# Opening of a fused attention and mixer kernel: smaller weight loads, more dummy products, one score moved

## The chip, the cores and the metric

The kernel runs on one core of a Trainium2 chip. The metric is the device time of one execution in microseconds (us), as the median of several runs. About 0.2% is the smallest difference that a measurement of this kernel tells from none.

## The reference

For each of 8 batches, attention over 12 heads with 448 tokens and 64 numbers a head, with a sigmoid in place of the softmax, and behind it a mixer block with two small networks, one over tokens and one over channels:

```python
scores = scale * np.matmul(q, k.transpose(0, 1, 3, 2)) - np.log(S)
attn = 1.0 / (1.0 + np.exp(-scores))
x = np.matmul(attn, v)                      # (8, 12, 448, 64), then (8, 448, 768)
h = np.maximum(x.transpose(0, 2, 1) @ w_tok1, 0.0) @ w_tok2
u = x + h.transpose(0, 2, 1)
h2 = np.maximum(u @ w_ch1, 0.0) @ w_ch2
return u + h2
```

`w_tok1` is 448 x 256, `w_ch1` 768 x 1536 and `w_ch2` 1536 x 768. Inputs and output are float32; the products are done in float16.

## The kernel before

The order of all work is written out by hand: the kernel's code lists the instructions, and each engine takes its own in that order. Semaphores for the data dependences are set by the framework.

The work goes in 24 cycles, three units (of four heads) for each of the 8 batches. A cycle computes seven scores with `qk(b, u, j)`: four products of 64 x 64 weights on TensorE into one of two score buffers in PSUM, then one sigmoid on ScalarE (L194) into `att`. Beside the scores of one unit stand the value products of the unit before (`av`), its transposition (`xtrans`, `xtrans_dma`), the token network (`tok1`, `ytrans`) and the channel network of the batch before (`ch1`, `ch2` and, from the third batch on, forms with fewer products).

The opening, about the first 64 us, differs from the steady part. Its pieces, in order:

- **Start.** `keep_warm(16)` gives TensorE 16 dummy products of 256 columns (the tile `heat`) while the first unit of `q` arrives. VectorE and ScalarE cast that unit (L1041, L1042). TensorE transposes `q` and the first two blocks of `k` (`tp_q`, `tp_k`), three more dummies follow, and the first scores start. Further `keep_warm` calls stand between the scores of cycle 0.
- **Cycles 0 to 2** (first batch) take their order from the list `between`. Behind them comes a stretch of single lines (L1102 to L1123) with cycle 3 (second batch, unit 0) and the first three blocks of `ch1`, the first product with `w_ch1`, held in `c1`. Of the six row blocks of `c1`, `ch1(0, cb, 0, 4)` uses blocks 0, 3, 1 and 4; blocks 2 and 5 follow in the loop at L1121.
- **Cycles 4 and 5** (second batch, units 1 and 2; the loop at L1146) hold the rest of `ch1` for the first batch. In each, `ch1_pair` does two blocks at once in 64-row steps: `turn0` has six steps of four products, `turn1` six more with the two PSUM banks swapped. Before the change the order is score 1, all of `turn0`, score 2, value products, score 3, value products, score 4, four steps of `turn1`, score 5, two steps, score 6. Cycle 5 ends with the first products that use `c2`, the other channel weight (L584). The transposed `q` and `k` of the third batch's units 1 and 2 are made in cycle 5 by VectorE copies (L129) and transposing DMAs on SP's queue (L142).

All loads of inputs and weights are issued by GpSimd (POOL), which casts them to float16 on the way, in one list (L945 to L1002). `load(b, t, src, u0, u1)` issues two transfers, one for each half of the partitions. The list goes: first batch; the token weights `w1` (two transfers, and one for its last 64 rows in partitions 0 to 63) and `w2s`; second batch's units with `load_c1(0)` (columns 0 to 767 of `c1`) and `load_c1(1)` among them; third batch's unit 0; `load_c2(0)`; third batch's units 1 and 2; `load_c2(1)`; third batch's first `v`. Partitions 64 to 127 of `w1`'s fourth block are set to zero first (L951) and loaded at L1189, in cycle 4. Later loads stand behind a small copy on POOL (`gate`, L1199, L1127, L1342), which waits for a transposing DMA or an output.

`turn_over(ps)` is a VectorE copy of one column from a PSUM bank; products into that bank that stand behind it in the order wait for it. It is used in the steady part, where a score stands within such steps.

Of the kernel before, what the change touches and what calls it, by code (L numbers as in the profile page):

```python
# [21 lines left out]
NJ = 7  # L22
NP = 64
NU = 3
# [6 lines left out]
def kernel(  # L31
# [11 lines left out]
    nc = tc.nc  # L43
# [5 lines left out]
    NDB = D // 128  # L49
    NCB = CC // 128  # L50
    N_CYCLES = NU * B
    N_FIRST = 4
# [13 lines left out]
    w1 = pc.tile([128, 4, TT], FP16, name="w1")  # L66
    w2 = pc.tile([128, 2, NJ, NP], FP16, name="w2")
    c1 = pc.tile([128, NDB, CC], FP16, name="c1")
# [12 lines left out]
    def xu(b):  # L81
        return xus[b % 2] if b else xu_0
# [5 lines left out]
    def bank(shape, dtype, name):  # L88

        if opening_banks:  # L90
            n = opening_banks.pop(0)
        else:
            n = at_bank[0]
            at_bank[0] = (n + 1) % 4
        return pp.tile(shape, dtype, tag=f"m{n}", bufs=1, name=name)
# [17 lines left out]
    def load(b, t, src, u0, u1):  # L113

        for g in range(2):
            dst = raw_tile(b, t)[64 * g : 64 * g + 64, u0:u1, :, :, :]
            heads = src[b, 6 * g + 2 * u0 : 6 * g + 2 * u1]
            nc.gpsimd.dma_start(
                out=dst.rearrange("p u hi j e -> p (u hi) (j e)"),
                in_=heads.rearrange("h (p j) e -> p h (j e)", j=NJ),  # L120
            )
# [60 lines left out]
    def qk(b, u, j):  # L182
        att[b, u, j] = pa.tile([128, 2, S], FP16, tag="att", bufs=10, name=f"att_{b}_{u}_{j}")
        ps = pp.tile([128, 2, 512], FP32, tag="qk", bufs=2, name=f"qk_{b}_{u}_{j}")
        for g in range(2):
            for hi in range(2):
                nc.tensor.matmul(  # L187
                    out=ps[64 * g : 64 * g + 64, hi, 0:S],
                    lhsT=tr[b, "k"][64 * hi : 64 * hi + 64, u, j, 64 * g : 64 * g + 64],
                    rhs=tr[b, "q"][64 * hi : 64 * hi + 64, u, :, 64 * g : 64 * g + 64],  # L190
                    start=True,
                    stop=True,
                )
        nc.scalar.activation(  # L194
            out=att[b, u, j][:, :, :],
            in_=ps[:, :, 0:S],
            func=SIGMOID,
            bias=bias_t[:, :],
            scale=att_scale,
        )  # L200
# [7 lines left out]
    def av(b, u, j0=0, j1=NJ, banks=None):  # L208
        if j0 == 0:
            xa[b, u] = banks or [  # L210
                bank([128, 512], FP32, f"xa_{b}_{u}_{g}")
                for g in range(2)
            ]
        ps = xa[b, u]
        for j in range(j0, j1):
            for g in range(2):
                for hi in range(2):
                    nc.tensor.matmul(  # L218
                        out=ps[g][64 * hi : 64 * hi + 64, 0:S],
                        lhsT=raw[b, "v"][64 * g : 64 * g + 64, u, hi, j, :],  # L220
                        rhs=att[b, u, j][64 * g : 64 * g + 64, hi, :],
                        start=(j == 0),
                        stop=(j == NJ - 1),
                    )
        if j1 == NJ:
            for g in range(2):
                nc.vector.tensor_copy(  # L227
                    out=xu(b)[:, u, g, 0:S], in_=ps[g][:, 0:S]
                )
            if NU * b + u >= N_CYCLES - 2:  # L230
                nc.vector.memset(xu(b)[:, u, :, S:512], 0.0)
            elif NU * b + u >= N_FIRST:
                nc.vector.tensor_copy(
                    out=xu(b)[:, u, :, S:512], in_=xu(b)[:, u, :, S - 64 : S]
                )
# [157 lines left out]
                    skip_group_check=loose,  # L393
                )

    def ch1_pair(b, cb):

        ps = [bank([128, 512], FP32, f"c1_{b}_{cb + p}") for p in range(2)]

        def step(turn, n):  # L400
            quads(
                ps,
                S,
                turn,
                lambda p, part, m: c1[
                    part, BY_UNIT[n], 128 * (cb + p) + m : 128 * (cb + p) + m + 64
                ],
                lambda p, part: ut(b, BY_UNIT[n])[part, 0:S],
                n == 0,
                n == NDB - 1,  # L410
            )

        def end():
            for p in range(2):
                ch1_out(b, cb + p, ps[p])

        turns = [[lambda t=t, n=n: step(t, n) for n in range(NDB)] for t in range(2)]
        return turns[0], turns[1], end
# [207 lines left out]
    turn_bank = {}  # L626
# [223 lines left out]
    def turn_over(ps):  # L850

        nc.vector.tensor_copy(out=turned[:, :], in_=ps[:, 0:1])
# [75 lines left out]
    for g, queue in enumerate((nc.scalar, nc.sync)):  # L928
        queue.dma_start(
            out=first_q[64 * g : 64 * g + 64].rearrange("p hi j e -> p hi (j e)"),  # L930
            in_=q[0, 6 * g : 6 * g + 2].rearrange("h (p j) e -> p h (j e)", j=NJ),
# [16 lines left out]
    nc.vector.memset(bias_t[:, :], att_bias)  # L948
    for b in range(2):
        nc.vector.memset(xu(b)[:, :, :, S:512], 0.0)  # L950
    nc.vector.memset(w1[64:128, 3, :], 0.0)  # L951
    load_first_k(2, NJ)
    load(0, "q", q, 1, 2)
    load(0, "k", k, 1, 2)
# [3 lines left out]
    tok_rows = moe_w_tok1.rearrange("(p j) t -> j p t", j=NJ)  # L958
    for par in range(2):
        part = slice(64 * par, 64 * par + 64)  # L960
        nc.gpsimd.dma_start(
            out=w1[part, 0:3, :],
            in_=tok_rows[0:6].rearrange("(t par) p c -> par p t c", par=2)[par],
        )
    nc.gpsimd.dma_start(out=w1[0:64, 3, :], in_=tok_rows[NJ - 1])
    load(0, "v", v, 1, 2)
    nc.gpsimd.dma_start(
        out=w2s[:, :, :], in_=moe_w_tok2.rearrange("(tc t) s -> t tc s", tc=2)
# [2 lines left out]
    load(1, "q", q, 0, 1)  # L971
    load(1, "k", k, 0, 1)

    def load_c1(half):
        cols = slice(CC // 2 * half, CC // 2 * half + CC // 2)
        nc.gpsimd.dma_start(
            out=c1[:, :, cols],
            in_=moe_w_ch1.rearrange("(db d) c -> d db c", db=NDB)[:, :, cols],
        )

    def load_c2(half):
        cols = slice(DH * half, DH * half + DH)
        nc.gpsimd.dma_start(
            out=c2[:, :, cols],
            in_=moe_w_ch2.rearrange("(cb c) d -> c cb d", cb=NCB)[:, :, cols],
        )

    load(1, "q", q, 1, 2)
    load(1, "k", k, 1, 2)
    load_c1(0)  # L990
    load(1, "v", v, 0, 1)
    load(1, "q", q, 2, NU)
    load(1, "k", k, 2, NU)
# [1 line left out]
    load(1, "v", v, 1, NU)  # L995
    load(2, "q", q, 0, 1)
    load(2, "k", k, 0, 1)
    load_c2(0)
    load(2, "k", k, 1, NU)
    load(2, "q", q, 1, NU)  # L1000
    load_c2(1)
    load(2, "v", v, 0, 1)  # L1002

# [22 lines left out]
    def keep_warm(n):  # L1026
        for _ in range(n):
            nc.tensor.matmul(
                out=heat[0][:, 0:256],
                lhsT=warm[:, 0:128],  # L1030
                rhs=warm[:, :],
                start=True,
                stop=True,
            )
# [1 line left out]

    nc.scalar.activation(out=gate[:, 0:1], in_=bias_t[:, :], func=SIGMOID)
    heat[0] = bank([128, 512], FP32, "heat")
    keep_warm(16)

    nc.vector.tensor_copy(out=raw_tile(0, "q")[:, 0, :, 0:4, :], in_=first_q[:, :, 0:4, :])  # L1041
    nc.scalar.activation(  # L1042
        out=raw_tile(0, "q")[:, 0, :, 4:NJ, :], in_=first_q[:, :, 4:NJ, :], func=COPYF
# [102 lines left out]
    for c, cb in ((N_FIRST, 3), (N_FIRST + 1, 8)):  # L1146
        b, u = divmod(c, NU)
        before = divmod(c - 1, NU)
        ahead = divmod(c + 1, NU)
        copies = []  # L1150

        def whole(cb):
            for d in range(0, NDB, 3):
                ch1(0, cb, d, d + 3)
                if copies:
                    copies.pop(0)()

        turn0, turn1, end = ch1_pair(0, cb)
        if c > N_FIRST:
            qk(b, u, 0)  # L1160
        qk(b, u, 1)
        for f in turn0:
            f()
        qk(b, u, 2)
        av(*before, 0, 4)
        qk(b, u, 3)
        av(*before, 4, NJ)
        if c - 1 in ON_DMA:
            xtrans_dma(*before)
        qk(b, u, 4)  # L1170
        for f in turn1[:4]:
            f()
        qk(b, u, 5)
        for f in turn1[4:]:
            f()
        end()
        qk(b, u, 6)
        if u == 2:
            copies = by_unit(2, 1)
        whole(cb + 2)  # L1180
        if c - 1 not in ON_DMA:
            xtrans(*before)
        for t in ("k", "q"):
            pe_transpose(ahead[0], t, ahead[1])
        whole(cb + 3)
        if c == N_FIRST:
            tok1(*before)
            whole(cb + 4)
            nc.gpsimd.dma_start(out=w1[64:128, 3, :], in_=tok_rows[NJ - 1])  # L1189
            ytrans(*before)  # L1190
        else:
            for w, f in pieces_ch2(0, by_half[:2]):
                f()
                if copies:
                    copies.pop(0)()
            while copies:
                copies.pop(0)()

            nc.gpsimd.tensor_copy(out=gate[:, :], in_=tr[2, "q"][:, 1, NJ - 1, 126:128])  # L1199
            load(2, "v", v, 1, NU)  # L1200
            gated_loads(b)
# [19 lines left out]
    for c in range(2 * NU, ONE_RUN):  # L1221
        b, u = divmod(c, NU)
# [170 lines left out]
    for c in range(ONE_RUN, N_CYCLES):  # L1393
        b, u = divmod(c, NU)
# [99 lines left out]
```

## Time and profile before

| | us |
|---|---|
| median of three runs | 341.08 |
| the runs | 341.34, 341.08, 340.71 |
| profiled execution | 341.39 |
| its span, first to last instruction | 339.6 |
| TensorE busy | 332.2 (98%) |
| ScalarE busy | 213.0 (63%) |
| VectorE busy | 234.9 (69%) |
| POOL busy | 58.7 (17%) |

The profile is of one execution, 341.39 us, of which 339.6 us lie between its first and last instruction. PE is TensorE's products, PEld its weight loads, DVE VectorE, ACT ScalarE, SP the queue of transposing DMAs and stores. A row of the timeline gives the start, the length, the engine, the line, the operation, its output and inputs and the number of instructions that were merged; in brackets stands how long the engine was idle before and what ended that. The ends of products are modelled, so rows of PE overlap a little.

### The profile page before, as it was taken

Reading aid. Unit: us, or ns where it says so; the run is one execution under the profiler, and the core shown is the slowest. Engines: PE = TensorE matmul, PEld = TensorE weight load, DVE = VectorE, ACT = ScalarE, POOL = GpSimd, SP = SyncE. Lnnn points to the kernel's source line nnn. Section 1 sums busy time; section 2 is a strip of 40 time slices with the busy share of each in tenths; the row PEclk is TensorE's granted clock in tenths of the full one; section 3 lists DMA queues with packets and bytes.
Section 4 is the critical chain, followed back from the end, with each engine's and each line's share of the span. In section 5 each row is a group of like instructions: output and inputs, shape, how many; then the busy total and the mean of one; then the engine's idle time right before and its main releaser. Section 6 shows DMA issues by size and latency. Waiting matters only on the chain.

```text
span 339.6 us, 10285 instructions
## 1 busy us (share of the span) xinstructions
PE 332.2 (98%) x4423; PEld 242.5 (71%) x4423; DVE 234.9 (69%) x484; ACT 213.0 (63%) x272; POOL 58.7 (17%) x102
## 2 busy tenths in 40 slices
PE   7999999999999999999999999999999999999994
PEld 4555565555796679866896679866896679769852
DVE  2277366678998973877768773878758654876882
ACT  3997657388647895578647895578647795314200
POOL 8981550050031000220032002020010000000000
PEclk9999999999999999999999999999999999999999
DMA  7999999999999999998999899988995293028007
GB/s 119 173 174 195 206 205 204 163 175 237 169 187 189 140 168 211 185 142 161 204 145 172 138 206 175 206 117 134 196 175 93 56 193 73 2 56 185 4 11 197
DMA packets 104381, 52.17 MB, mean 154 GB/s; under 512 B 76432, under 2 KB 101264, under 8 KB 104336
## 3 DMA queue, kind: packets, MB, share of 16 engines
q1 hardware_dynamic: 78704, 29.11, 47.8%
q0 software_dynamic: 25168, 21.50, 42.1%
q10 hardware_dynamic: 464, 0.92, 1.0%
q8 instruction: 34, 0.56, 0.7%
q14 instruction: 11, 0.09, 0.1%
HBM read 43.45 MB, written 11.01 MB: 160 GB/s over the span
## 4 chain that ended last, share of the span: by engine, by line
PE 86%; DMA 5%; POOL 4%; ACT 2%; issue 1%; DVE 0%; ACTq 0%; POOLq 0%
PE c_ab L514 14%; PE c L814 10%; PE qk L187 9%; PE c_c L514 8%; PE xa L218 7%; PE c L861 6%; PE tk L296 5%; PE yt L316 5%; PE c L387 4%; DMA c<-in_moe_w_ch_dram 4%; PE c L584 4%; PE c L364 3%; PE c L669 3%; PE c L650 2%; ACT att L194 2%; DMA raw_v<-in_v_dram 2%
## 5 line engine op out<-in xcount | busy, mean ns | idle before, releaser
L194 ACT ACTIVATE att<-qk,att_bias 128x896 f16<-128x896 f32 x168 | 156.0, 1012 | 38.6 <-PE qk L187 37.6
L187 PE MATMUL qk<-tr_q,tr_k 64*64 64x448 f16 x672 | 61.3, 360 | 0.3 <-ACT att L194 0.2
L514 PEld LDWEIGHTS <-c 128*128 128x128 f16 x504 | 48.4, 98 | 1.1 <-issue 0.3
L218 PE MATMUL xa<-att,raw_v 64*64 64x448 f16 x644 | 40.7, 349 | 0.0
L187 PEld LDWEIGHTS <-tr_k 64*64 64x64 f16 x672 | 25.2, 105 | 19.0 <-issue 11.9
L514 PEld LDWEIGHTS <-sum 128*128 128x128 f16 x378 | 36.3, 98 | 0.0
L227 DVE CAST xu<-xa 128x448 f16<-128x448 f32 x40 | 23.1, 619 | 18.8 <-PE xa L218 18.4
L535 ACT ACTIVATE pt_ab<-c_ab 128x896 f32<-128x896 f32 x21 | 19.2, 917 | 20.6 <-PE c_ab L514 20.6
L218 PEld LDWEIGHTS <-raw_v 64*64 64x64 f16 x672 | 22.0, 107 | 8.3 <-issue 0.4
L861 PE MATMUL c<-c,h 64*64 64x384 f16 x360 | 24.6, 322 | 0.0
L1127 POOL COPY gate<-tr_q 128x2 f16<-128x2 f16 x6 | 1.6, 275 | 121.7 <-DMA tr_q<-rel_q 121.7
L326 DVE TENSOR_TENSOR xu<-xu,yt 128x448 f16<-128x448 f16 x38 | 21.7, 613 | 0.0
L537 ACT ACTIVATE h<-c_ab 128x896 f16<-128x896 f32 x7 | 6.4, 917 | 24.4 <-PE c_ab L514 24.4
L296 PE MATMUL tk<-xn,w 128*128 128x256 f16 x156 | 21.2, 274 | 0.1
L544 DVE TENSOR_TENSOR h<-pt_ab,c_ab 128x896 f16<-128x896 f32 x14 | 15.2, 1084 | 8.6 <-PE c_ab L514 8.6
L544 DVE TENSOR_TENSOR h<-pt_c,c_c 128x448 f16<-128x448 f32 x21 | 12.9, 614 | 11.7 <-PE c_c L514 11.6
L316 PE MATMUL yt<-w,h 128*128 128x448 f16 x88 | 20.3, 353 | 0.0
L841 DVE TENSOR_TENSOR o<-un,c 128x384 f32<-128x384 f16 x32 | 17.4, 550 | 4.0 <-PE c L814 4.0
L310 ACT ACTIVATE h<-tk 128x256 f16<-128x256 f32 x42 | 14.2, 406 | 9.5 <-PE tk L296 9.5
L814 PEld LDWEIGHTS <-hid 128*128 128x128 f16 x132 | 12.9, 98 | 8.0
L514 PE MATMUL c_ab<-diffs,c 128*128 128x224 f16 x168 | 18.4, 259 | 0.0
L296 PEld LDWEIGHTS <-w 128*128 128x128 f16 x156 | 13.6, 98 | 5.7 <-issue 2.4
(134 smaller groups left out, 572.1 us busy)
## 6 DMA issues: line engine op xcount, KB each, us to landing
out_dram<-o SPq DMA_DIRECT2D x41, 192.0 KB, 3.2
c<-in_moe_w_ch_dram POOLq DMA_DIRECT2D x4, 1152.0 KB, 16.1
raw_k<-in_k_dram POOLq DMA_DIRECT2D x10, 336.0 KB, 6.9
raw_q<-in_q_dram POOLq DMA_DIRECT2D x10, 336.0 KB, 5.7
raw_v<-in_v_dram POOLq DMA_DIRECT2D x10, 336.0 KB, 8.8
out_dram<-o SPq DMA_DIRECT2D x15, 96.0 KB, 2.4
raw_q<-in_q_dram POOLq DMA_DIRECT2D x12, 112.0 KB, 5.1
raw_k<-in_k_dram POOLq DMA_DIRECT2D x12, 112.0 KB, 5.4
```

Of the source, the lines that this page charges most:

```text
L187: nc.tensor.matmul(out=ps[64 * g : 64 * g + 64, hi, 0:S], lhsT=tr[b, "k"][64 * hi : 64 * hi + 64, u, j, 64 * g : 64 * g + 64], rhs=tr[b, " ...
L194: nc.scalar.activation(out=att[b, u, j][:, :, :], in_=ps[:, :, 0:S], func=SIGMOID, bias=bias_t[:, :], scale=att_scale,)
L218: nc.tensor.matmul(out=ps[g][64 * hi : 64 * hi + 64, 0:S], lhsT=raw[b, "v"][64 * g : 64 * g + 64, u, hi, j, :], rhs=att[b, u, j][64 * g : ...
L227: nc.vector.tensor_copy(out=xu(b)[:, u, g, 0:S], in_=ps[g][:, 0:S])
L296: nc.tensor.matmul(out=ps[tcb], lhsT=w1[rows, t, cols], rhs=xn[b, u][rows, :, t, :], start=(t == 0 and not with_scores), stop=(t == (2 if ...
L316: nc.tensor.matmul(out=ps[:, 0:S], lhsT=h1[b, u][:, tcb, g, :], rhs=w2[:, tcb, :, :], start=(tcb == 0), stop=(tcb == 1),)
L326: nc.vector.tensor_tensor(out=x, in0=x, in1=ps[:, 0:S], op=ADD)
L514: nc.tensor.matmul(out=ps[:, g, p, :], lhsT=weights[n][:, d, 128 * cb : 128 * cb + 128], rhs=moving[n][:, d, :], start=(n in (1, 5, 2) and ...
L535: nc.scalar.activation(out=shaped(part[:, :, :]), in_=ps, func=COPYF)
L544: nc.vector.tensor_tensor(out=shaped(dst), in0=shaped(parts[gs, which]), in1=ps, op=ADD)
L814: nc.tensor.matmul(out=ps[:, 0:DH], lhsT=self.weights[n][:, k, :], rhs=self.moving[n][:, k, :], start=(n in (1, 2, 5) and k == 0), stop=(k ...
L861: nc.tensor.matmul(out=ps[m : m + 64, 0:DH], lhsT=lhsT(n)[part, m : m + 64], rhs=rhs(n)[part, :], start=(opens and turn == 0 and n == 0), ...
```

## The change

Five things, all in the opening:

1. The first half of `c1` is loaded in three transfers, each with two of the six row blocks (0 and 3, 1 and 4, 2 and 5), the first ahead of the second batch's unit 1 of `q` and `k`, the others behind it. Before, it was one transfer behind them.
2. `keep_warm(21)` in place of `keep_warm(16)` at the start.
3. In cycle 4, score 2 stands behind the third step of `turn0`, not behind the sixth. `turn_over` on the second bank is added behind score 3, and the group check of these products is off.
4. The third batch's unit 1 of `k` and `q` is loaded ahead of the first half of `c2`, unit 2 behind it. Before, units 1 and 2 came together behind it.
5. The last rows of `w1` are loaded into both halves of the partitions at the start; the fill with zeros (L951) and the load in cycle 4 (L1189) are gone.

```diff
-    def ch1_pair(b, cb):
+    def ch1_pair(b, cb, loose=False):
         ps = [bank([128, 512], FP32, f"c1_{b}_{cb + p}") for p in range(2)]
+        turn_bank[0] = ps[1]
...
                 n == 0,
                 n == NDB - 1,
+                loose,
             )
...
-    nc.vector.memset(w1[64:128, 3, :], 0.0)
...
-    nc.gpsimd.dma_start(out=w1[0:64, 3, :], in_=tok_rows[NJ - 1])
+    for half in range(2):
+        nc.gpsimd.dma_start(
+            out=w1[64 * half : 64 * half + 64, 3, :], in_=tok_rows[NJ - 1]
+        )
...
-    def load_c1(half):
+    def load_c1(half, u=None):
         cols = slice(CC // 2 * half, CC // 2 * half + CC // 2)
+        blocks = slice(0, NDB) if u is None else slice(u, NDB, NU)
         nc.gpsimd.dma_start(
-            out=c1[:, :, cols],
-            in_=moe_w_ch1.rearrange("(db d) c -> d db c", db=NDB)[:, :, cols],
+            out=c1[:, blocks, cols],
+            in_=moe_w_ch1.rearrange("(db d) c -> d db c", db=NDB)[:, blocks, cols],
         )
...
+    load_c1(0, 0)
     load(1, "q", q, 1, 2)
     load(1, "k", k, 1, 2)
-    load_c1(0)
+    load_c1(0, 1)
+    load_c1(0, 2)
...
     load(2, "k", k, 0, 1)
+    load(2, "k", k, 1, 2)
+    load(2, "q", q, 1, 2)
     load_c2(0)
-    load(2, "k", k, 1, NU)
-    load(2, "q", q, 1, NU)
+    load(2, "k", k, 2, NU)
+    load(2, "q", q, 2, NU)
...
-    keep_warm(16)
+    keep_warm(21)
...
-        turn0, turn1, end = ch1_pair(0, cb)
+        turn0, turn1, end = ch1_pair(0, cb, loose=(c == N_FIRST))
...
-        for f in turn0:
+        for f in turn0[:3]:
             f()
-        qk(b, u, 2)
+        if c == N_FIRST:
+            qk(b, u, 2)
+        for f in turn0[3:]:
+            f()
+        if c > N_FIRST:
+            qk(b, u, 2)
         av(*before, 0, 4)
         qk(b, u, 3)
+        if c == N_FIRST:
+            turn_over(turn_bank[0])
         av(*before, 4, NJ)
...
-            nc.gpsimd.dma_start(out=w1[64:128, 3, :], in_=tok_rows[NJ - 1])
```

## The prediction

> **What bounds the kernel now.** I read the page's busy times first (PE 98%), then the waits and the timeline by engine up to 66 us, then the chain of waits there. TensorE is the limit nearly everywhere: its waits come to 2.5 us in the whole span, and the first two lie ahead of the first transpose.
>
> ```profile
> PE tp_q L170 <- DVE raw_q L1041: 1.2, 1, 1.2
> PE heat L1028 <- DVE att_bias L948: 1.1, 1, 1.1
> PE qk L187 <- ACT att L194: 0.2, 1, 0.2
> ```
>
> So a shift gained in the opening should reach the end unshortened, unless a transfer that doesn't move with it becomes late. The timeline of PE shows three places where time is lost:
>
> ```profile
> 1.05 3.59 PE L1028 MATMUL heat<-warm 128*128 128x256 f16 x16 [1.05 <-DVE att_bias L948]
> 5.83 0.96 PE L170 MATMUL tp_q<-ident,raw_q 128*64 128x128 f16 x14 [1.18 <-DVE raw_q L1041]
> 6.93 0.82 PE L1028 MATMUL heat<-warm 128*128 128x256 f16 x3
> 7.68 0.96 PE L187 MATMUL qk<-tr_q,tr_k 64*64 64x448 f16 x8
> 10.48 0.61 PE L1028 MATMUL heat<-warm 128*128 128x256 f16 x4
> 11.34 0.58 PE L170 MATMUL tp_q<-ident,raw_q 128*64 128x128 f16 x14
> ...
> 44.42 0.38 PE L187 MATMUL qk<-tr_q,tr_k 64*64 64x448 f16 x4 [0.16 <-ACT att L194]
> ```
>
> First, speed: one dummy of 256 columns follows the other after (3.59 - 0.42) / 15 = 0.21 us up to 9.9 us (0.42 is the length of one), but after about 0.11 us from 10.48 on; 14 transposes take 0.96, later 0.58. TensorE works at half speed until about 10.4 us, though the granted clock of the page reads full from the start. Second, the wait for `c1`, in the weight loads and in the chain (start, length, what):
>
> ```profile
> 33.70 0.49 PEld L364 LDWEIGHTS <-c 128*128 128x128 f16 x4 [0.41 <-DMA c<-in_moe_w_ch_dram]
> ```
>
> ```profile
> 21.01 12.64 DMA c<-in_moe_w_ch_dram
> 33.65 0.05 issue
> 33.70 0.93 PE c L364 x4
> ...
> 44.42 0.38 PE qk L187 x4
> ...
> 48.64 0.87 PE tk L296 x8
> ```
>
> Third, the last row of the timeline: score 6 of cycle 4 waits for a sigmoid. And ScalarE's timeline says what carries the early speed onward:
>
> ```profile
> 8.33 1.91 ACT L194 ACTIVATE att<-qk,att_bias 128x896 f16<-128x896 f32 x2 [1.01 <-PE qk L187]
> 10.61 19.58 ACT L194 ACTIVATE att<-qk,att_bias 128x896 f16<-128x896 f32 x21 [0.38 <-PE qk L187]
> ...
> 41.34 4.83 ACT L194 ACTIVATE att<-qk,att_bias 128x896 f16<-128x896 f32 x5 [0.51 <-PE qk L187]
> ```
>
> From 10.61 on 21 sigmoids stand back to back, about 0.9 us apart: scores that start sooner move all of cycles 0 to 2.
>
> **The change, part by part.**
>
> *21 dummies.* Five more at 0.21 us end at about 5.5 us, still ahead of the transposes at 5.83, so they delay nothing; the gap ahead of the transposes falls from 1.4 to 0.3 us. What they buy is an earlier rise of the speed. The trace bounds when: 3.4 us of dummies alone (1.05 to 4.4) did not raise it, 4.6 us of nearly unbroken work (5.83 to 10.4) did. With 21, work is nearly unbroken from 1.05, so 4.6 us of it are over at about 6. The earliest is 1.05 + 3.4 = 4.5, the latest 10.4 as now. At full speed before 5.8: transposes 0.38 shorter, so the copies of `q` and `k` end at about 7.0 and the first score starts there and not at 7.68; its products end 0.2 sooner, the first sigmoid starts near 7.45 and not at 8.33, the second follows at once, and the third, now kept waiting 0.38 by slow transposes of `k`, starts near 9.26: 1.35 sooner. If the speed rises only at 7.0, the same steps give a third sigmoid at 9.6: 1.0 sooner. I take 1.2 (ends 0 and 1.35). Data allow it: by the trace of DMA issues the second unit's `k` lands at 10.7, its transpose would move from 13.0 to 11.8.
>
> [...]
>
> *`c1` in thirds.* At 32.54 start eight products (`tk`) that take 0.87 elsewhere (chain, 48.64), so `ch1` could start at 33.41 and starts at 33.70: 0.29 gained if `c1` is there. It must now be there 1.2 sooner, at 32.2. The page of transfers gives about 200 GB/s; a third is 384 KB, 1.9 us. The first third stands ahead of unit 1 and should land near 25, the second near 30, two products later than the first in use; the third third near 33, needed by the loop at L1121, now at 38.1. Unit 1 of `q` and `k` moves back behind the first third: from 23.7 and 25.9 to about 28, needed at 31.48 - 1.2 = 30.3. POOL pays two more issues of 0.6 to 0.84 us; it is 17% busy. If this cover were gone, up to the shift itself is lost.
>
> *Score 2 of cycle 4.* It moves three steps forward, 3 x 0.19 us (24 products from 39.54 to 40.71). Its sigmoid then starts when the one before ends, about 40.75 and not at 41.34. Score 3 keeps its place on PE, so the next sigmoid starts at 42.1 for 42.28, and the fifth (score 4) at 43.0 for 43.37; score 6 finds its buffer at 44.05 for 44.42. Modelled ends put the wait at 0.16; counted from 43.55 with 8 products at 0.049 it is 0.48. I take 0.3. `turn_over` costs 0.16 us (its median at L852, where it already runs) on a VectorE that is idle from 40.7 to 42.6; behind it stand the copies of the value products, which wait for PE until 42.6 anyway, and the four steps of `turn1` wait for it from 42.6. It costs nothing; without the idle time 0.16.
>
> *Third batch's unit 1 ahead of `c2`, `w1` early, no fill.* One transfer of 32 KB moves from 54.11 to 12.2 on POOL (issue 0.55, so what is behind it comes up to 0.55 later); the next user, unit 1 of `v`, landed 3.5 us ahead of its use. Four pieces of 112 KB pass `c2`'s first half, which so lands 4 x 0.57 = 2.3 us later, near 56 for 53.6; L584 needs it at 60.09 - 1.8. Four further issues cost POOL 2.4 us. The copies at L129 get unit 1 sooner, and they did not wait before. The fill is 0.17 us on an idle VectorE. Together nothing.
>
> Sum: 1.2 + 0.3 + 0.3 = 1.8 us. The profiled execution had 341.39 (span 339.6 and 1.8 around it), so 339.6; it lies 0.3 above the median of the runs, whose own sum gives 339.3. I say 339.5.
>
> **Rivals.**
>
> *The speed does not rise sooner* (0.14). If transposes don't count as work, the dummies up to 5.5 are followed by a break until the next dummies at 6.93: 1.4 us, as long as the idle time that stands there now (4.4 to 5.83). The speed then rises at 10.4 as before, the first term is 0, and 0.6 us remain: 340.8 by the profiled execution, 340.5 by the median. Against it: the stretch from 6.93 to 10.4, at whose end the speed did rise, holds 0.74 us of transposes and some 0.6 us of waits. [...]
>
> *`c2`'s first half comes late* (0.06), the one that ends slower. Each POOL transfer waits for the landing of the eighth before it:
>
> ```profile
> 33.94 1.24 POOL L118 DMA_DIRECT2D raw_v<-in_v_dram  x2 [6.74 <-DMA c<-in_moe_w_ch_dram]
> ```
>
> That `v` is eighth behind `c1`. In the new list `c2`'s first half is eighth behind a piece that lands at 45.8, so it is issued at about 46, not 37.58. Were it to keep its 16.0 us to landing, it would land at 62 for a need at 58.3: 3.8 lost, 1.8 gained, 343.4. It decides against the change from a landing at 60.8 on. Against it: those 16 us are the queue ahead of it, at about 200 GB/s all the way, and that queue is as long in either list but for four pieces.
>
> *A transposing DMA caps the shift* (0.10). `xn` of cycle 4, issued on SP at 56.30, lands at 66.4 behind the loads, and `tk` (L277) uses it at 68.4; the next is issued at 68.31, lands at 74.8, used near 76.7. Loads don't move with PE. After 1.8 us the margins are 0.2 and 0.1. With half a us of disturbance the shift ends at 1.2: 340.0.
>
> **From cases to numbers.** The forecast has 0.67, other mishaps 0.03. About 0.2%, 0.7 us, is what a measurement of this kernel can tell from no change. Faster by more: the forecast, the cap and a little of the first rival, 0.79; within: the rest of that, 0.13; slower 0.08. Range: the forecast with its ends reaches from 338.9 (1.95 off the lowest run shown gives 338.8) to 340.1, the cap is inside, and the first rival's 340.5 is taken in: 338.9 to 340.6.
>
> **What would show it.** In the new profile: dummies after about 6 us 0.11 apart; the third sigmoid near 9.4; no idle time ahead of the first product with `c1`, near 32.2; score 6 of cycle 4 without a wait near 42.6; L584 with no wait for `c2`; `tk` near 66.6 with none for `xn`. Dummies still 0.21 apart at 9 us, or a PE wait over 0.5 us for a DMA after 30 us, would prove it wrong.

## The result and the profile after

The changed kernel takes 342.64 us (median of 22 runs, 341.27 to 344.35) against 341.12 for the kernel before in the same series (22 runs, 339.71 to 342.33): ratio 1.0046, interval 1.0031 to 1.0061. It is slower by 0.46%, where 339.5 was forecast. A second series gave 342.03 against 341.01, ratio 1.0030 (1.0009 to 1.0051). The profiled execution took 342.46 (span 340.6), 1.07 more than that of the kernel before. Ratios leave out executions that lay over 1.5% above the fastest of their kernel, the medians don't.

The opening did what was said. Timeline of PE (start, length, what), the rows that answer to the first and third views of the kernel before, and the one row of ScalarE's:

```profile
1.06 4.66 PE L1037 MATMUL heat<-warm 128*128 128x256 f16 x21 [1.06 <-DVE att_bias L950]
5.82 0.70 PE L170 MATMUL tp_q<-ident,raw_q 128*64 128x128 f16 x14
6.36 0.28 PE L170 MATMUL tp_k<-ident,raw_k 128*64 128x128 f16 x4
6.57 0.50 PE L1037 MATMUL heat<-warm 128*128 128x256 f16 x3
...
42.85 0.38 PE L187 MATMUL qk<-tr_q,tr_k 64*64 64x448 f16 x4 [0.16 <-ACT att L194]
```

```profile
7.54 4.60 ACT L194 ACTIVATE att<-qk,att_bias 128x896 f16<-128x896 f32 x5 [0.48 <-PE qk L187]
```

The dummies end at 5.72 and delay nothing; three of them take 0.50 from 6.57 on, where three took 0.82 before. The transposes come 0.11 us apart, in pairs, up to 6.04 and 0.056 apart from 6.14 on: the speed doubles at about 6.1, not 10.4. The third sigmoid starts at 9.34 for 10.61, 1.27 sooner. The first product with `c1` has no idle time ahead of it. Score 6 of cycle 4 starts at 42.85 for 44.42, 1.57 sooner, but its wait is still there.

From then on the gain is given back. The waits of PE between 60 and 120 us, of which the kernel before has none that this view lists:

```profile
PE c_ab L516 <- DVE h L546: 1.0, 1, 1.0
PE c L863 <- DVE turned L854: 0.7, 1, 0.7
PE c_c L516 <- DVE h L546: 0.4, 1, 0.4
```

The view counts from the modelled end of the product ahead. Counted from where the next one would have started at the spacing of the products ahead, as PE's waits are in the text from here on, they are 0.61 us at 93.25, 1.21 at 99.06 and 0.83 at 114.32: 2.65 together, against a single 0.28 us at 89.03 before. 1.57 gained, 2.37 lost, 0.8 to the bad; the span is 1.0 longer. What PE waits for stands on VectorE, and VectorE waits for loads. Its timeline, first before, then after (in brackets its idle time ahead and what ended it):

```profile
81.29 1.67 DVE L129 COPY rel_k<-raw_k 128x896 f16<-128x896 f16 x3
84.76 0.62 DVE L129 COPY rel_q<-raw_q 128x896 f16<-128x896 f16 x1
```

```profile
82.08 1.67 DVE L129 COPY rel_k<-raw_k 128x896 f16<-128x896 f16 x3 [2.28 <-issue]
86.25 0.62 DVE L129 COPY rel_q<-raw_q 128x896 f16<-128x896 f16 x1 [1.21 <-DMA raw_q<-in_q_dram]
...
112.18 0.62 DVE L129 COPY rel_k<-raw_k 128x896 f16<-128x896 f16 x1 [0.81 <-issue]
```

Where a bracket names no releaser but "issue", it is a load, too: the fourth batch's `k` lands at 82.00 and the fifth's at 112.10, each 0.08 us ahead of its copy. The token sums behind these copies start at 88.44 for 86.95. And the chain of waits of the changed kernel says who hands on to whom:

```profile
60.92 9.45 DMA tr_q<-rel_q
70.43 0.18 POOL gate L1214
...
74.51 11.72 DMA raw_q<-in_q_dram
86.25 0.62 DVE rel_q L129
...
92.29 6.48 DMA tr_q<-rel_q
...
98.89 0.02 POOL gate L1136
...
102.37 9.00 DMA raw_k<-in_k_dram
112.18 0.62 DVE rel_k L129
...
114.20 0.08 DVE turned L854
114.32 0.52 PE c L863 x8
```

This is a relay. A transposing DMA on SP lands; a gate on POOL opens and the next batch's `k` and `q` are loaded; VectorE copies them; SP transposes them; the next gate opens. No link of it waits for PE. But VectorE does other work for PE in between and in order, and SP's stores and transposing DMAs, which an earlier PE lets start sooner (the four stores of `out_first` at 76.08 to 78.76 for 77.61 to 80.34), are under way together with the loads (from 80 to 84 us 515 packets on SP's queue beside 521 of the loads). It came later by this much (from the DMA issues of the two traces): `c2`'s second half lands at 66.02 for 64.53, the third batch's `q` is transposed at 70.37 for 67.85, the fourth batch's `q` is loaded at 86.23 for 82.49, the fifth's `k` at 112.10 for 109.68. Part of the first comes from the new list. The rate of transfer in slices of 1 us from 36 to 76 us, before and after:

```profile
GB/s 213 210 209 202 203 201 201 207 200 201 206 207 205 202 210 195 204 201 207 198 205 207 203 211 190 181 140 80 64 103 255 279 151 10 183 192 202 248 195 201
```

```profile
GB/s 209 210 214 206 212 197 202 203 197 202 161 136 170 193 198 205 207 207 195 201 203 213 194 184 191 189 192 192 194 135 67 152 238 6 232 254 110 82 169 188
```

From 46 to 50 us some 160 KB are missing, 0.8 us at 200 GB/s, about half of the 1.49. POOL issued nothing from 37.28 to 42.58 because the eighth transfer before was `c1`'s second half (5.30 us idle, ended by its landing), and `c2`'s first half followed at 44.84 for 37.58: for a while only pieces of 112 KB were under way. In the kernel before POOL stands still at the same place, up to 42.90, but has issued `c2`'s first half ahead of it. All nine profiled executions with the new order of these loads have such a gap between 44 and 54 us (slowest slice 93 to 154 GB/s), and none of the eleven without it (192 and more).

### The profile page after: what moved, and what is told of

The parts are those of the page before. It is cut to its first block, busy times and chain, and to the rows that moved or that the text cites. A ratio compares the mean times of both kernels' runs of the same rounds, so it can differ in the third digit from the quotient of the medians.

```text
span 340.6 us, 10303 instructions
## 1 busy us (share of the span) xinstructions
PE 332.2 (98%) x4428; PEld 243.5 (71%) x4428; DVE 234.6 (69%) x484; ACT 213.0 (63%) x272; POOL 61.7 (18%) x108
## 4 chain that ended last, share of the span: by engine, by line
PE 75%; DMA 12%; ACT 5%; DVE 3%; issue 2%; POOL 1%; POOLq 0%; DVEq 0%; ACTq 0%
PE c_ab L516 12%; PE c L816 10%; PE qk L187 8%; PE c_c L516 7%; PE xa L218 6%; PE c L863 5%; PE tk L296 5%; DMA tr_q<-rel_q 5%; ACT att L194 5%; PE c L387 4%; PE yt L316 4%; DMA raw_q<-in_q_dram 3%; PE c L671 3%; PE c L364 3%; DMA raw_k<-in_k_dram 3%; PE c L652 2%
## 5 line engine op out<-in xcount | busy, mean ns | idle before, releaser
L863 PEld LDWEIGHTS <-h 64*64 64x64 f16 x360 | 14.4, 107 | 5.2 <-issue 0.9
```

The lines of the kernel that those rows point to most:

```text
L863: nc.tensor.matmul(out=ps[m : m + 64, 0:DH], lhsT=lhsT(n)[part, m : m + 64], rhs=rhs(n)[part, :], start=(opens and turn == 0 and n == 0), ...
```

## The experiments

Series of 12 runs (6 with one load moved, 13 in the last), each with the kernel before beside it. Executions of one kernel differ by 2 to 5 us; a table below shows what they differ in. So the profiled executions carry the reasoning, and the times only say whether it adds up.

**One part undone or alone.** *Without the swap* (third batch's unit 1 back behind `c2`'s first half):

```
-    load(2, "k", k, 1, 2)
-    load(2, "q", q, 1, 2)
     load_c2(0)
-    load(2, "k", k, 2, NU)
-    load(2, "q", q, 2, NU)
+    load(2, "k", k, 1, NU)
+    load(2, "q", q, 1, NU)
```

> The changed kernel with part 4 undone: the third batch's units 1 and 2 of k and q come together behind the first half of c2 again; everything else as changed. Theory A (the new place of these pieces breaks the flow of loads: POOL stands from 37 to 42.6 us, the DMA engines run short at 46 to 49 us, and all later loads are some 1 to 4 us late): no dip at 46 to 49 us, the second half of c2 lands near 64.5, the third batch's transposed q near 68, the fourth batch's q near 82.5, no waits of PE over 0.4 us between 86 and 116; 1.3 to 1.6 us faster than before the change. Theory B (loads do not move with PE at all, and an earlier PE issues the transposing DMAs into the second half of c2, so that both get late whatever the list): the same waits as in the changed kernel, 0 to 1.5 us slower than before.

340.72 against 340.95, ratio 0.9996 (0.9979 to 1.0013), where theory A had 1.3 to 1.6 us less than before; profiled 340.33, 1.06 less. The gap in the rate is gone, `q` lands at 82.28, and VectorE finds it there:

```profile
83.48 0.62 DVE L129 COPY rel_q<-raw_q 128x896 f16<-128x896 f16 x1
```

*The swap alone*, put into the kernel before:

> The kernel before with part 4 alone. Theory A: the dip at 46 to 49 us appears, the fourth batch's q lands 2 to 4 us later than 82.5, VectorE waits for it; some 1 to 2.5 us slower than before. Theory B: PE is not earlier, so the transposing DMAs are not issued sooner, and the time stays within 0.7 us of before.

341.31, ratio 1.0011 (0.9996 to 1.0025): the gap that theory A forecast is there (100 GB/s from 48 to 49 us), and the time is theory B's. The loads are as late as in the changed kernel (`c2` 66.00, `q` 85.42), VectorE waits 0.30 us for `q`, and PE has no wait that the kernel before hasn't.

*The changed kernel with 16 dummies*, and *the kernel before with 21*:

```
-    keep_warm(21)
+    keep_warm(16)
```

> The changed kernel with 16 dummy products. Theory A: the late loads set the end, so the opening's 1.2 us matter little: within 0.7 us of the changed kernel, 1 to 1.5 us slower than before. Theory B: PE is no longer early, the mixing goes, and the time is within 0.7 us of before.

> The kernel before with 21 dummy products alone. By both theories the first scores start about 1.2 us sooner, and the first product with c1 still waits for its whole first half, which lands at 33.65 in the profile of before: the idle time there grows from 0.3 to about 1.5 us, and the total stays within 0.5 us of before.

341.31 (1.0007, 0.9987 to 1.0027) and 341.46 (1.0015, 0.9988 to 1.0041). With 16 the third sigmoid is back at 10.31, `q` lands at 85.47, and PE has one new wait (0.61 us at 76.55, for `xn`), none from 90 to 115. With 21 alone the third sigmoid starts at 9.33, the wait for `c1` grows to 0.62 (1.5 was expected, but `c1` landed at 32.69, not at 33.65), and PE has no wait after 60 that the kernel before hasn't. So in these profiled executions late loads alone cost little, early PE alone costs nothing, and both together make the 2.65 us of waits. But the one with 21 alone, 340.58, is the second fastest of its 12, and what the others waited for no trace shows. The next runs showed that this wasn't all.

**VectorE's order.** The token sums, which stood behind the copies of `q`, go ahead of them:

```
         if c == 2 * NU + 2:
+            token_sums(b - 1)
             copies += through_dma(3, 0)[NU + 1 :]
...
             utrans(b - 1)
-            token_sums(b - 1)
```

> The changed kernel, with one thing moved on VectorE alone: the token sums of the third batch (L459, four operations) stand ahead of the copies of the fourth batch's q (L129) and not behind them. Theory (the loss is paid on VectorE, whose instructions run in order: it stands still for the fourth batch's q, 1.21 us ahead of 86.25, everything behind it, the token sums at 88.44 first, is late, and PE waits 0.61 us at 93.25 and 1.21 us at 99.06): the sums then run in that idle time, near 85.0 to 87.0, the wait for q falls from 1.2 us to about nothing, the two PE waits together from 1.82 us to 0.6 or less, and the time by about 1.2 us, from 342.5 to 341.3; the PE wait near 114 (0.83 us, for the fourth batch's next k) can stay. Rival (PE waits for late transfers themselves, or for the later c2 and v, and VectorE's order is no part of it): the waits at 93 and 99 stay at 1.8 us and the time at 342.5.

The place was right and the time wrong: 343.95, ratio 1.0049 (1.0011 to 1.0087). VectorE's wait for `q` falls to 0.23 and the waits at 93 and 99 are gone, as forecast. PE is then early at 111.7 and waits there longer, 2.31 us. Waits of PE from 60 to 120:

```profile
PE c L863 <- DVE turned L854: 2.2, 1, 2.2
```

The fifth batch's `k` lands at 111.65, 0.45 sooner than in the changed kernel, and most of the two earlier waits comes back here. But the waits together are no longer than the changed kernel's, and the profiled time, 343.89, is 1.43 above its 342.46. That is paid behind the wait, in TensorE's clock. From the table of windows (length, busy time of PE, granted clock, share and rate of DMA):

```profile
113.90:116.00 2.10, 2.10 (x32) 0.56 1.33 118
116.00:118.00 2.00, 2.00 (x20) 0.60 1.35 176
```

What the clock lost there is 0.44 x 2.1 + 0.40 x 2.0 = 1.7 us of work (an estimate; more in the last section).

**One load moved.** The third batch's `v` of unit 2 behind the fourth batch's `k` and `q`:

```
-            load(2, "v", v, 1, NU)
+            load(2, "v", v, 1, 2)
             gated_loads(b)
+            load(2, "v", v, 2, NU)
```

> The changed kernel, with the third batch's v for unit 2 loaded behind the fourth batch's k and q and not ahead of them (one piece per half moves on POOL's queue). Theory (the fourth batch's k and q are late on the same queue, and that is what VectorE stands still for): they land about 1.2 us sooner (q near 85.0 for 86.23), the wait of the copies of q falls from 1.2 us to about 0, the PE waits at 93 and 99 from 1.82 us to 0.6 or less; time near 341.3 against 342.5 for the changed kernel, unless the v that is now later stops PE itself. Rival (the loss comes from c2 and the third batch's own loads, which stay where they are): no change, 342.5.

Wrong: 346.11 (6 runs), ratio 1.0139 (1.0097 to 1.0180). `q` landed at 86.89, no sooner. This execution lost 1.8 us already at 23.7 and 26.1, where PE waited for the second batch's `q` and `k`, and `c2`'s second half came at 67.76; so it doesn't test the move by itself. It does show the price of a long wait (last section).

**The same move of the sums without the swap, and a second try at cycle 4.**

> The changed kernel with the third batch's unit 1 back behind c2's first half, and the token sums ahead of the copies of q. Theory: without the swap the copies of q did not wait (83.48, no idle time ahead), so the move of the sums has nothing to fill, and the time is that of the kernel without the swap, about 340.4 profiled and 340.7 median. Rival (the sums ahead of q make q's transposing DMA 2 us later and that stops PE): 341.5 or more.

> The kernel before this one (no swap, sums first), and in cycle 4 score 3 is issued ahead of the four value steps, too. Theory of the missing 0.3 us in cycle 4 (score 2 came sooner, but its sigmoid only ends the wait of the next one: score 3 stayed where it was and its sigmoid can't start before its products end): now the sigmoids of scores 2, 3 and 4 follow each other without the idle 0.5 us, and PE's wait ahead of score 6 falls from 0.32 us to 0.1 or less; the time by up to 0.25 us, to about 340.2 profiled. Rival (the wait is a delay of the semaphore between ScalarE and PE, not ScalarE's order): 0.32 stays, the time stays.

342.41 (1.0021, 0.9981 to 1.0062), in two groups: six runs from 339.73 to 341.34, six from 343.49 to 346.01, where 340.7 was forecast. The profiled execution, 340.12, is of the first group and has no wait after 60 beyond the 0.28. With score 3 ahead of the value steps as well, nine of 12 runs lie at 339.81 to 341.11 and three at 344.6 to 347.2 (median 340.13; ratio 0.9987, 0.9956 to 1.0019). But the wait ahead of score 6 was 0.31 us still. The profiled one is the longest, 347.15: though it is without the swap, PE waits 3.98 us at 116.38, and the granted clock is 0.50 up to 120 us and 0.58 from 120 to 122.

**The amount to be loaded.** The second half of `c2` copied on chip, and a useless load ahead of it:

```
-    load_c2(1)
     load(2, "v", v, 0, 1)
+    for n in range(0, NCB, NCB // 4):
+        blocks = slice(n, n + NCB // 4)
+        nc.gpsimd.tensor_copy(out=c2[:, blocks, DH : 2 * DH], in_=c2[:, blocks, 0:DH])
```

> The changed kernel, swap and all, but the second half of c2 (1.18 MB, some 5.9 us at 200 GB/s) isn't loaded: POOL copies the first half there, so the products of that half have other values and the same shapes. Theory (the queue of loads and transposing DMAs is full from 8 to 110 us and is the second bound of this stage; PE's earlier start only uses up the distance to it): the transposing DMAs of the third batch land near 62 to 66 and not at 68.2 to 71.9, the fourth batch's q before 83, VectorE doesn't stand still for it, PE has no wait over 0.3 us after 60, and the 1.57 us of the opening reach the end: span near 338.0, 339.8 with what lies around it. Rival 1 (what costs is the swap itself, the eight-place wait on POOL, which is unchanged): 342.5. Rival 2 (PE is slowed by something else after the opening): 341 or more with waits that aren't for loads.

340.56, ratio 1.0004 (0.9961 to 1.0047); nine of 12 runs at 339.80 to 341.18, three at 344.88. The profiled one is of the three. Its transposing DMAs land at 62.5 to 66.0, `q` at 79.78, as forecast, and yet PE waits 3.74 us at 79.72, for another link. From its chain:

```profile
67.46 12.21 DMA xn<-xu
79.72 0.30 PE tk L277 x4
```

`xn` was issued on SP as the fourth batch's loads were issued on POOL, and landed with the last of them. So relieving one link let the loads collide with another.

```
+    nc.gpsimd.dma_start(
+        out=sums[2][:, :, :],
+        in_=moe_w_ch1.rearrange("(db d) c -> d db c", db=NDB)[:, 0:NU, 0 : CC // 2],
+    )
     load_c2(1)
```

> The kernel before, with PE's opening as it was, and one useless load of 590 KB (2.9 us at 200 GB/s) on POOL's queue ahead of c2's second half. Theory (late loads cost as soon as they pass PE by some 2 us, whichever of the two moved): c2's second half lands near 67.4 for 64.5, the fourth batch's q near 85 to 86 for 82.5, VectorE stands still for it near 85, and PE waits near 95 or near 114 by 1 to 3 us in all: 342.5 to 344.5. Rival (it is the early PE that provokes it, by issuing transposing DMAs into the loads): 341.1, as before.

344.90, ratio 1.0067 (1.0026 to 1.0108). `c2` landed at 68.80 and `q` at 89.45, later than forecast, and most of the price was paid at a place that no theory had named, 2.10 us at 70.47:

```profile
PE tk L277 <- DMA w<-in_moe_w_tok_dram: 1.9, 1, 1.9
```

That is the transfer of 32 KB into `w1`, which the changed kernel issues at 12 us. In the order of before it stands behind `c2`, lands at 66.17 there and at 70.43 here. Behind that wait, too, the granted clock falls, to 0.64 from 70.4 to 72.4 and 0.51 from 72.4 to 74.4. So late loads cost 3 us and more with PE's old opening too, about 1.7 of it by the clock, but the run is a poor stand-in for the swap: of its waits only the 0.58 us at 117.60 is the changed kernel's.

**Without the swap once more**, with score 3 moved and as it was:

> The changed kernel without the swap, VectorE's order as it was, and score 3 of cycle 4 ahead of the value steps. With the score moved the wait ahead of score 6 stays at 0.31 us (it did in the run with both moves), so the time is that of the kernel without the swap: 340.2 to 340.7. If the move had worth of its own, 0.25 us less.

> The changed kernel without the swap, a second time, beside the others on the same chip: 340.7, no PE wait over 0.3 us after 60 in the profiled execution. If the earlier PE alone is enough to meet the loads, some of its runs lie 3 us and more higher, as a quarter of those of the kernel with score 3 moved did.

342.06 (1.0008, 0.9972 to 1.0043) and 342.10 (1.0006, 0.9973 to 1.0039). The same kernel that had given 340.72 now gives 342.10, and its profiled execution, 342.80, has waits like the changed kernel's without its swap:

```profile
PE c L863 <- DVE turned L854: 1.4, 1, 1.4
```

With score 3 moved the profiled execution waits, too, 0.86 us at 98.00 and 1.30 at 113.73. So early PE is enough without the swap when the loads happen to be late, and the swap is not the whole cause.

**One link shortened.** On SP, the first batch's third output tile is stored behind the transposing DMA of `q`, not ahead of it (line numbers behind this place are 5 higher in the kernels that have it):

```
+    held_back = []
-    def store(b, t):
+    def store(b, t, now=False):
+        if (b, t) == (0, 2) and not now:
+            held_back.append(lambda: store(b, t, True))
+            return
...
             copies += through_dma(3, 0)[NU + 1 :]
+            copies.append(lambda: [f() for f in held_back])
```

> The changed kernel again, beside the next three on the same chip: 342.6 median as before, with PE waits near 93, 99 and 114 in the profiled execution, 2.6 us together, and the fourth batch's q landing near 86.

> The changed kernel with one thing moved on SP alone: the two stores of the first batch's third output tile (L623, out<-o, issued at 90.12 to 92.19) stand behind the transposing DMAs of the fourth batch's q (L142) and of un (L343), not ahead of them. Relay theory: tr_q is issued near 90.1 for 92.29 and lands near 96.6 for 98.77, the gate (L1136) opens 2 us sooner, the fifth batch's k lands near 110 for 112.1, and PE's wait near 114 (0.83 us) goes; the waits near 93 and 99, which hang on the landing of the fourth batch's q, stay: 341.7 against 342.5. VectorE's order or the swap alone: no change, 342.5.

> The changed kernel with both moves: token sums ahead of the copies of q on VectorE (alone it only moved PE's wait to 114) and the two stores behind tr_q on SP. Relay theory: the wait near 114 falls from 2.3 us to 0.5 or less and those near 93 and 99 stay away, so the gain of the opening reaches the end with the swap in place: span 338.3 to 338.8, 340.1 to 340.6 in all. The swap alone: 342.5 or more.

> The same two moves without the swap. Relay theory: the wait near 114 has 2 us more room, so the runs that lay at 343.5 to 346 (half of them with the sums moved alone) come down to 340 to 341: median 340.2, below the kernel before (341.0) by 0.2%. Otherwise two groups of runs stay, at 340 and at 344.

The changed kernel gave 342.03 (told above), with waits of 0.58, 1.21 and 1.09. With the stores behind: 341.86, ratio 1.0002 (0.9974 to 1.0030), profiled 341.79 for a forecast of 341.7. `tr_q` is issued at 90.10 and lands at 96.23, the fifth batch's `k` lands at 111.39 for 112.34, the wait at 114 is 0.23, and the others stay, in the list of waits:

```profile
PE c_ab L516 <- DVE h L546: 1.0, 1, 1.0
PE c_c L516 <- DVE h L546: 0.2, 1, 0.2
```

That is the relay's forecast, but for the `k`, which was to land near 110. With the sums moved too, the swap in place, the profiled execution (341.31) has no wait after 60 beyond 0.28, as forecast; it waits 1.70 us at 24.39 for the second batch's `q`. It is the second fastest of its 12; the series lies at 344.07 (1.0080, 1.0050 to 1.0111), not at 340.1 to 340.6, and what its other runs waited for no trace shows. Without the swap and with both moves: 340.37 against 341.01, ratio 0.9980 (0.9955 to 1.0005).

> The version without the swap, with the sums ahead of q's copies and the two stores behind tr_q, a second time. Relay theory: no PE wait over 0.3 us after 56 in the profiled execution and a median of 340.4, the lower group of the kernel without the swap. If the first series was luck, 341.5 or more with the wait at 114 back.

> The kernel before with the two moves alone (sums ahead on VectorE, stores behind tr_q on SP). Relay theory: there PE is 1.3 to 1.6 us later and the relay was on time anyway (one wait of 0.28 us after 60 us), so the moves free nothing: 341.0, as before. If the two moves are what makes the best version quick, it comes down to 340.4 as well, and the opening is worth nothing.

The second series of that version: 341.80 against 341.42, ratio 0.9996 (0.9960 to 1.0032), in two groups again, eight runs from 339.99 to 341.97 and four from 344.3 to 345.3. So no version is shown to beat the kernel before. The two moves in the kernel before give 341.19 (0.9982, 0.9959 to 1.0006), as forecast, though its profiled execution has a wait of 1.64 us at 77.69 for `xn`.

**What two executions of one kernel differ in.** Three kernels were profiled twice. Both executions of the changed kernel are long; of the other two kernels each pair holds one short and one long execution. Times of landing by the DMA issues, in us; the last two columns are PE's waits after 60 us (over 0.2 us) and the whole execution:

| kernel | score 6, cycle 4 | `c2`, 2nd half | third `q` transposed | fourth `q` loaded | fifth `k` loaded | waits | time |
|---|---|---|---|---|---|---|---|
| before | 44.43 | 64.53 | 67.85 | 82.49 | 109.68 | 0.28 | 341.39 |
| changed | 42.85 | 66.02 | 70.37 | 86.23 | 112.10 | 2.65 | 342.46 |
| changed, again | 42.87 | 64.92 | 69.41 | 86.22 | 112.34 | 2.87 | 342.74 |
| no swap | 43.15 | 63.77 | 66.73 | 82.28 | 108.14 | 0.28 | 340.33 |
| no swap, again | 43.63 | 65.54 | 69.58 | 85.53 | 112.30 | 2.19 | 342.80 |
| no swap, both moves | 43.00 | 63.85 | 66.97 | 82.08 | 107.88 | 0.28 | 339.98 |
| the same, again | 42.67 | 65.18 | 69.62 | 85.92 | 112.17 | 4.29 | 344.40 |
| swap only | 44.85 | 66.00 | 69.08 | 85.42 | 111.07 | 0.28 | 341.98 |

In those two pairs `c2`'s second half comes 1.3 to 1.8 us later, the transposed `q` 2.7 to 2.9, the next `q` 3.3 to 3.8: the relay enlarges a small delay. The landing of `c2` isn't the whole of it, though: in the changed kernel's second execution it is only 0.39 later than before, and `q` as late as in the first. In the pair without the swap the delay begins in the opening (POOL's 20th transfer is issued at 13.35 and at 15.16, just behind the landing of its 12th at 13.06 and 14.87); why that one lands when it does stays open.

## Why the prediction was wrong

**The opening: right.** 1.2 us were forecast for the dummies and 1.27 came; the rise of the speed at "about 6" came at 6.1. That it was 6.1 is chance: in the 15 profiled executions with 21 dummies the speed doubles between 3.9 and 6.6 us, in the five with 16 between 9.3 and 12.2, so 4.5 wasn't the earliest that it could be, against the prediction's working, and the 7.0 of its late case is in none of the 15. The third sigmoid starts at 9.31 in the mean of the 15 and at 10.48 in that of the five, 1.17 apart, so the size holds. 0.3 for `c1` in thirds was right (0.29), its thirds landing at 26.4, 30.6 and 32.7. The rival in which the speed doesn't rise fell. Whether transposes count as work isn't shown: 4.66 us of dummies stood ahead of them here. The 1.57 us up to score 6 hold for the profiled pair. Over all profiled executions score 6 of cycle 4 starts at 44.26 with 16 dummies (mean of 5) and at 43.20 with 21 and thirds (mean of 14), 1.06 apart: five of the 14 waited 0.65 to 1.83 us between 23 and 27 for the second batch's `q` and `k`, which the earlier PE reaches before they land.

**Score 2: a term that wasn't there.** 0.3 was forecast, 0 came: the wait is 0.319 us for 0.318. The step counted 0.45 us from the issue of score 3 to its sigmoid. It is 0.63 (issued at 40.08, sigmoid at 40.71), as it was for score 2 in the profile of before (40.71 and 41.34). And it took the sigmoid of score 4 to start sooner because the ones ahead do. It doesn't hang on them: in all 20 profiled executions it starts 0.95 to 0.96 us after score 4's own issue (42.41 and 43.37 before, 40.84 and 41.80 after), and score 6 starts 1.06 after that. With score 3 moved as well ScalarE stands idle 0.64 us ahead of this sigmoid (issued at 40.73, sigmoid at 41.69), and PE's wait is 0.31. Neither move changes the place of score 4 ahead of score 6, so neither can shorten the wait. Why score 4 takes 0.96 where the two ahead of it take 0.63 stays open.

**The failed step: "a shift gained in the opening should reach the end unshortened", and with it "Third batch's unit 1 ahead of `c2` ... Together nothing".** Of the 1.57 us gained up to score 6 nothing reached the end. The relay of loads, transposing DMAs and copies, which doesn't move with PE, became late, and PE lost 2.37 us to it. The landing of `c2`'s first half was forecast "near 56" and came at 56.06, and L584 didn't wait. But the edit was priced at that first use alone. Behind `c2` landed the transposing DMAs (its second half at 64.53 and the transposed `q` at 67.85 before, 66.02 and 70.37 after), and behind them stood the relay. Its margins stood in the trace of before: the fourth batch's `q` landed at 82.49 for a copy at 84.76, 2.27 to spare, and the fifth's `k` at 109.68 for 111.04, 1.36. `q` came 3.74 later and PE 1.57 sooner, 5.31 against 2.27; `k` 2.42 later, 3.99 against 1.36 if PE isn't stopped ahead of it. The prediction had looked for such margins at `xn` alone (0.2 and 0.1). Where the relay was on time the shift did reach the end: without the swap a profiled execution gained 1.28 us up to score 6 and 1.06 in all, and with both moves besides 1.43 and 1.41. But those are single executions, and no series shows a gain beyond its interval.

**The rivals.** The one that ended slower had part of the cause in it: the row in which a transfer waits for the eighth before it. POOL did stand still for it, and the rate fell. It was priced at the wrong place (L584, where PE didn't wait) and given 0.06; that its 343.4 is nearer to 342.64 than the forecast is luck. The rival with `xn` named the right kind of link; its own wait is absent from the changed kernel's profile and costs 0.6 to 3.7 us in four of the experiments' (16 dummies, `c2` copied, and the two moves with and without the opening). The chance of 0.79 for a gain rested on a sum that had no term for what the loads do after 56 us.

**What is shown and what isn't.** Shown: that the waits of the profiled executions come from the relay (the chain; each shortened link moved the next wait, mostly as forecast), that the swap leaves a gap in the transfers, and that a wait of 2 us and more can cost half as much again or more by the clock (an estimated 1.7 us on top of 2.31 and of 2.98). Likely: that early PE and the swap each use up part of one margin; 1 of 34 runs of the changed kernel lies below 341.0, 11 of 36 without the swap (the series with score 3 moved among them), and of the kernel before's between 15 of 35 and 18 of 35 in the same series. Not shown: how much of the 0.46% is the swap's, since the series without it scatter from 340.72 to 342.10; what the thirds of `c1`, score 2 and the early `w1` add, none of which was undone alone; why a series with both moves in the changed kernel lies at 344.07; and what makes the early loads land late in one execution and not in another.

## What to carry to other kernels

An engine at 98% can still stand a microsecond or two away from a second bound (here 1.36 and 2.27 us). Before a shift is credited to the end, list every transfer that doesn't move with it and the margin of each, as landing against first use, and follow what its landing releases: here a delay of 0.4 to 1.5 us had grown to 3.7 two links further on. When one wait is removed, look for the next one on the same chain. And where executions of one kernel differ by more than the effect, profile it twice: the pairs showed more than the medians did.

## What the runs showed of the hardware

**A transposing DMA among queued loads.** In the changed kernel, with loads queued, the four transposing DMAs of the third batch take until the loads are through: issued from 56.6 on, landed from 68.2 on, while the loads move 220 packets from 64 to 68 us and none from 68 to 72. With the second half of `c2` copied, one issued beside four loads took 12.2 us (the chain above), another in the same execution, issued at 89.60 with no load under way, 3.1. How the two queues share the transfer is counted in the changed kernel's trace: from 56 to 60 us, with both issued, 949 packets of the loads and 210 of SP's, from 60 to 64 us 748 and 751. Whether SP's queue had work on every DMA engine all that time isn't shown.

**A wait can cost more than its length.** In the kernel with `v` moved PE waited 2.98 us ahead of 117.20. The table of windows (length, busy time of PE, granted clock, share and rate of DMA):

```profile
114.00:117.20 3.20, 0.38 (x9) 1.00 1.86 64
117.20:119.00 1.80, 1.74 (x32) 0.84 1.10 112
119.00:121.00 2.00, 1.93 (x11) 0.50 1.33 185
121.00:123.00 2.00, 2.00 (x10) 0.79 1.16 273
```

At half clock products of 128x384 came 0.32 us apart for 0.16, and about 1.7 us went on top of the wait (0.16 x 1.8 + 0.50 x 2 + 0.21 x 2). The same fall stands behind waits of 2.31 us (sums first), 2.10 (the useless load) and 3.98 (score 3 with the sums). Behind waits of 2.80 (both moves without the swap, second time) and 3.74 (`c2` copied) the granted clock stayed at 1.00. So in these traces the length of a wait doesn't decide it alone; what else does isn't shown.
